# Start and tail of a two-problem attention kernel: x transposed on TensorE, a new order of the first projections and batches, more PSUM banks for the last output tiles

## The chip, the core and the metric

The kernel runs on one core of a Trainium2 chip. The metric is the time of one execution on the device in microseconds. Three runs of the kernel before took 801.57, 802.39 and 803.64 us; the median is 802.39. One execution was also recorded by the hardware profiler.

A core has five engines, each with its own instruction stream: TensorE (PE) multiplies matrices and writes to PSUM, VectorE (DVE) and ScalarE (ACT) read PSUM and compute, GpSimd (POOL) works in SBUF, and SyncE (SP) here only issues DMAs. PSUM has eight banks. A bank holds 128 x 512 numbers in f32. In the profile PEld is the loading of a matmul's stationary operand.

## The reference

Two independent problems, A and B, have the same shapes. For each of them, in bf16:

```python
B, Sq, D = 16, 80, 576
Hq, Hkv, Sk, Dh = 32, 16, 512, 128
q = (x @ wq).reshape(B, Sq, Hq, Dh).transpose(0, 2, 1, 3)
k = jnp.repeat(k_cache, 2, axis=1)
v = jnp.repeat(v_cache, 2, axis=1)
scores = jnp.einsum("bhqd,bhkd->bhqk", q, k) * (Dh ** -0.5)
p = softmax(scores, axis=-1)
o = jnp.einsum("bhqk,bhkd->bhqd", p, v)
result = o.transpose(0, 2, 1, 3).reshape(B, Sq, Hq * Dh) @ wo
```

The two results are joined along the last axis. Softmax goes over 512 keys, and two query heads share one key head.

## The kernel before, in words

**Units.** Work is cut into 128 units `U`, 64 a problem. A unit is one batch (80 rows of x) and four key heads, thus eight query heads. Eight units make an octet `goct` with one piece of 1024 columns of wq. A problem has four pieces `q` and two halves of eight batches (640 rows of x, `half` 0 and 1), so eight octets. The order is problem, piece, half, batch.

**Steps of a unit.** Q projection (line 454): for each of an octet's eight heads `i`, five matmuls over the depth of x give the transposed Q of up to six batches at a time. In octet 0 a head is cut into batches 0 and 1 (`c` = 0, 160 columns) and the other six (`c` = 1, 480 columns). In later octets the cut is six batches and then two. ACT or DVE moves the result to `qT` (465, 466). Scores: each key head has 160 query rows. The first 128 go through one matmul of 512 keys (558). The 32 rows left over of the four heads are packed side by side into one bank by four column-tiled matmuls (544, `qkr`). So a unit has five score tiles, k = 0 being the packed one. DVE takes the maximum (567), ACT the exponential and the row sum (571), DVE one reciprocal for a unit (577), POOL multiplies (580), PE transposes the tile with four matmuls (586), DVE moves it to `pT` (592, 594), PE multiplies by V (624) and ACT moves the result to `oT` (639).

**Pairs.** `qk_order` (496 to 500) puts units in groups of `GR` = 2: first the packed tiles of both, then the four tiles of the first and of the second. One `qkr` operation holds the packed matmuls of both units, so it waits for both K loads.

**Output.** After two pieces of wq the product with 16 heads of wo is formed: 20 tiles of 128 x 288, sixteen matmuls each, in two operations of eight (669). For the first two pieces ACT copies a tile to `acc` (681). For the last two DVE adds tile and `acc` into one of two `osb` slots (696), and SP writes it to the result (702). All these tiles use the one PSUM bank of class `M`.

**Loads.** SP issues x by transposing DMAs straight into `xT` (390 and 395; a half is split into rows 0 to 159 and 160 to 639, and each part into four chunks of depth and a last one), K by transposing DMAs into six slots (513), V into four (517), wo in four pieces (490), and the later wq. ACT issues the wq of octet 0 in two pieces of 512 columns (428, 431).

**What sets the order.** Every operation has a stream, an engine, a key and an assumed duration. The planner (`_Sched.arrange`, 97) simulates the engines with these durations. Each time an engine is free it takes, among the heads of its streams that are ready in the simulation, the one with the lowest key. It also hands out PSUM banks: from the class's list in `BANKS` (25) it takes the one that became free first. The resulting order on each engine is fixed in the program; on the chip every operation waits on semaphores for its real inputs. Before all this, PE runs eight matmuls on constants (`em_warm`, 361).

In octet 0 the keys let all eight `c` = 0 groups go first, then the `c` = 1 groups mixed with the first groups of octet 1, which read half 1 of x.

Of the kernel before, what the change touches and what calls it, by code (L numbers as in the profile page):

```python
# [6 lines left out]
BF16 = mybir.dt.bfloat16  # L7
F32 = mybir.dt.float32
AF = mybir.ActivationFunctionType
AX = mybir.AxisListType  # L10

GR = 2
LA = 9
NK = 6
# [5 lines left out]
QSH = 10  # L20
NOC = 2
NOSB = 2
NWARM = 8
NWC = 4
BANKS = dict(S=(0, 1, 2, 6), T=(3, 4), O=(5,), M=(7,), M0=(7, 5, 6, 3, 4), M1=(7, 6))
XDMA = True
RG = ((0, 1, 2, 3, 4),)
NSS = 6
OPSPLIT = 2
OP0 = 20.0  # L30
OPS = 1.25
LP0 = 20.0
# [6 lines left out]
def _mm(n, cols):  # L39
    return n * (cols * MM1 + MM0)  # L40
# [239 lines left out]
def bass_concat_heads__gqa_block_cached__gqa_block_cached__near_ridge_kernel(  # L280
# [5 lines left out]
    probs = [  # L286
        (A_x, A_k_cache, A_v_cache, A_wq, A_wo),
        (B_x, B_k_cache, B_v_cache, B_wq, B_wo),
    ]
    B, SQ, D = A_x.shape  # L290
    _, G, SK, DH = A_k_cache.shape
# [4 lines left out]
    NPP = B // 8  # L296
    NG = 2 * NOCT * NPP
    UPR = NOCT * NPP * 8
    NSU = 2 * UPR
# [3 lines left out]
    NROW = 8 * SQ  # L303
    NRT = NROW // 128
# [3 lines left out]
    with ExitStack() as es:  # L308
# [3 lines left out]
        ones = sb("ones", [128, 128], BF16)  # L312
# [26 lines left out]
        def R(res, ver):  # L339
            return (res, ver)  # L340
# [26 lines left out]
        def em_warmend(e):  # L367
# [3 lines left out]
        S.add("pe", -990, em_warm, reads=[R(("ones",), 0), R(("warm",), 0)], writes=[R(vw, 0)],  # L371
              name="warm", stream="W", dur=NWARM * 0.427, alloc=[vw])
        S.add("dve", -980, em_warmend, reads=[R(vw, 0)], writes=[R(("warm",), 1)], name="warmend", stream="warmset")
        IDENT = R(("ident",), 0)

        def unit(g):
# [1 line left out]
            q, half = divmod(r, NPP)  # L378
            return prob, q, half

        XB = ((0, 160), (160, 640))
        for prob in range(2):
            x_ap = probs[prob][0]
            for half in range(NPP):
                for part in range(2):
                    r0, r1 = XB[part]

                    def em_ldx(e, x_ap=x_ap, half=half, r0=r0, r1=r1):
                        src = x_ap.rearrange("b s d -> (b s) d")[half * NROW + r0:half * NROW + r1, :]
                        return e.dma_start_transpose(xT[:, half, 0:4, r0:r1],  # L390
                                                     src[:, 0:512].rearrange("n (c d) -> n c d", c=4))

                    def em_ldx4(e, x_ap=x_ap, half=half, r0=r0, r1=r1):
                        src = x_ap.rearrange("b s d -> (b s) d")[half * NROW + r0:half * NROW + r1, :]
                        return e.dma_start_transpose(xT[:, half, 4:5, r0:r1],  # L395
                                                     src[:, D - 128:D].rearrange("n (c d) -> n c d", c=1))

                    k_ = 5.0 * (prob * UPR + 8 * half - QSH) - 20.0 + 0.2 * part
                    if prob == 0:
                        k_ = ((-100.0, -60.0), (-45.0, -44.9))[half][part]  # L400
                    nr = (r1 - r0) / 640.0
                    S.add("sp", k_, em_ldx, writes=[R(("xT", half, part, 0), prob)], dsem="d_x%d%d" % (half, part),
                          name="ldx%d.%d.%d" % (prob, half, part), stream="x", dur=4.4 * nr + 0.3, cost=3.5 * nr)
                    S.add("sp", k_ + 0.01, em_ldx4, writes=[R(("xT", half, part, 1), prob)],
                          dsem="d_x%d%d" % (half, part), name="ldx4%d.%d.%d" % (prob, half, part), stream="x",
                          dur=1.1 * nr + 0.3, cost=0.9 * nr)

        QB = ((0, 6), (6, 2))
        for goct in range(NG):
# [30 lines left out]
            for i in range(8):  # L440
                for c in range(2):
                    if goct == 0:
                        b0, nb = ((0, 2), (2, 6))[c]
                        x = (-LA - 6.0 + 0.6 * i) if c == 0 else (-LA + 0.5 + 1.2 * i)
                    else:
                        b0, nb = QB[c]
                        x = 5.0 * (u0 - QSH + i) + (3.6 if c == 0 else 1.6)
                    n0, n1 = b0 * SQ, (b0 + nb) * SQ
                    vb = S.bank("M0" if goct == 0 else "M1" if goct == 1 else "M")

                    def em_qp(e, i=i, wsl=wsl, half=half, n0=n0, n1=n1, vb=vb):
                        last = None
                        for ck in range(5):
                            last = e.matmul(ps[:, vb.phys, 0:n1 - n0],  # L454
                                            lhsT=wq_sb[:, wsl, ck, i * 128:(i + 1) * 128],
                                            rhs=xT[:, half, ck, n0:n1], start=(ck == 0), stop=(ck == 4))
                        return last

                    col = (i // 2) * 160 + (i % 2) * 80

                    def em_qev(e, en, qsl=qsl, b0=b0, nb=nb, n0=n0, n1=n1, col=col, vb=vb):
                        dst = qT[:, qsl, b0:b0 + nb, col:col + 80]
                        src = ps[:, vb.phys, 0:n1 - n0].rearrange("p (b s) -> p b s", b=nb)
                        if en == "act":
                            return e.activation(dst, src, AF.Identity, scale=SCALE)  # L465
                        return e.tensor_scalar(dst, src, SCALE, None, op0=AluOpType.mult)  # L466

                    xr = [R(("xT", half, p_, h_), prob) for p_ in range(2) for h_ in range(2)
                          if n0 < XB[p_][1] and n1 > XB[p_][0]]
                    S.add("pe", x, em_qp,  # L470
                          reads=[R(("wq", wsl, s_, i // 4), wv) for s_ in "ab"] + [R(("wqz",), 0)] + xr,
                          writes=[R(vb, 0)], name="qp%d.%d.%d" % (goct, i, c), stream="Q",
                          dur=_mm(5, n1 - n0), lat=0.2, alloc=[vb])
                    big = n1 - n0 > 200
                    S.add(("act", "dve"), x + 0.4, em_qev, reads=[R(vb, 0)],
                          writes=[R(("qT", qsl, bl, i), goct) for bl in range(b0, b0 + nb)],
                          name="qev%d.%d.%d" % (goct, i, c), stream="qev",
                          dur=dict(act=0.47, dve=0.57) if big else dict(act=0.21, dve=0.23))
# [15 lines left out]
                          dsem="d_wo", name="ldwo%d.%d.%d" % (prob, hh, wc), stream="wo", dur=0.5, cost=2.0)  # L494

        qk_order = []
        for p_ in range(NSU // GR):
            qk_order += [(GR * p_ + j_, 0) for j_ in range(GR)]
            qk_order += [(GR * p_ + j_, k_) for j_ in range(GR) for k_ in range(1, 5)]
        Qof = dict((uk, i_) for i_, uk in enumerate(qk_order))  # L500
        vbs = {}
        group = []
# [1 line left out]
        for U in range(NSU):  # L504
# [10 lines left out]
            def em_ldv(e, vc_ap=vc_ap, b=b, q=q, vs=vs):  # L515
                src = vc_ap[b, 4 * q:4 * q + 4, :, :].rearrange("g (p j) d -> p g (j d)", j=4)
                return e.dma_start(v_sb[:, vs, :, :], src)

            S.add("sp", 5.0 * (U - U % GR) + 0.5 * (U % GR) - LA - 8.0, em_ldk, writes=[R(("kT", ks), U)],
                  dsem="d_k%d" % ks, name="ldk%d" % U, stream="K", dur=3.4, cost=2.75)  # L520
            S.add("sp", 5.0 * U - 6.0, em_ldv, writes=[R(("V", vs), U)],
                  dsem="d_v%d" % vs, name="ldv%d" % U, stream="V", dur=0.45, cost=1.6)
# [2 lines left out]
            for k in range(5):  # L525
# [10 lines left out]

                if k == 0:
                    group.append((U, vb, ks, qsl, bl, goct))
                    if len(group) == GR:
                        def em_qkr(e, group=tuple(group)):  # L540
                            last = None
                            for _, vb_, ks_, qsl_, bl_, _ in group:
                                for g4 in range(4):
                                    last = e.matmul(ps[32 * g4:32 * g4 + 32, vb_.phys, :],  # L544
                                                    lhsT=qT[:, qsl_, bl_, g4 * 160 + 128:g4 * 160 + 160],
                                                    rhs=kT[:, ks_, :, g4 * 128:(g4 + 1) * 128],
                                                    start=True, stop=True, tile_position=(0, 32 * g4))
                            return last

                        S.add("pe", Qof[(group[0][0], 0)] - LA + 0.0, em_qkr,  # L550
                              reads=[R(("qT", g_[3], g_[4], i), g_[5]) for g_ in group for i in (1, 3, 5, 7)]
                              + [R(("kT", g_[2]), g_[0]) for g_ in group],
                              writes=[R(g_[1], 0) for g_ in group], name="qkr%d" % U, stream="S",
                              dur=GR * (_mm(1, 512) + 0.0105), lat=0.2, alloc=[g_[1] for g_ in group], mode=1)
                        group = []
                else:
                    def em_qk(e, gl=gl, vb=vb, ks=ks, qsl=qsl, bl=bl):
# [89 lines left out]
        for prob in range(2):  # L647
            for hh in range(NPAIR):
                for half in range(NPP):
                    for n in range(NB_):  # L650
# [6 lines left out]
                        else:  # L657
                            x = 5.0 * (base + OP0 + OPS * (half * NB_ + n)) + 0.6
                        slot = (half * NB_ + n) % NOSB
                        vb = S.bank("M")  # L660
                        ver = (prob, hh)
                        ot_reads = [R(("oT", half, b_, q_, pr_), ver) for b_ in bls for q_ in range(2)
                                    for pr_ in range(2)]
# [15 lines left out]
                        if hh == 0:  # L679
                            def em_ea(e, rb=rb, c3=c3, vb=vb):  # L680
                                return e.copy(acc[:, rb, c3 * DC:(c3 + 1) * DC], ps[:, vb.phys, 0:DC])

                            S.add("act", xe, em_ea, reads=[R(vb, 0)],
                                  writes=[R(("acc", rb, c3), ver)], name="oea%d.%d.%d" % (prob, half, n),
                                  stream="oea", dur=0.30)
                        elif not last:
                            def em_em(e, rb=rb, c3=c3, vb=vb):
# [94 lines left out]
```

## Time and profile before

| What | us |
|---|---|
| median of three runs | 802.39 |
| the profiled execution's own time | 802.79 |
| its span, first to last instruction | 801.0 |
| PE busy (8200 matmuls) | 783.7 (98%) |
| DVE busy | 685.3 (86%) |
| ACT busy | 614.4 (77%) |
| POOL busy | 431.9 (54%) |
| PE's mean granted clock | 0.998 of full speed |
| DMA queues' packets, share of 16 engines | about 89% |
| first projection / first score on PE starts at | 8.81 / 25.89 |
| last unit's transposes, last V product end near | 778.4 / 780.2 |

Matmuls are pipelined, and their ends are modelled: a busy PE is not always a PE at its peak. The chain of work that ended last is followed back from the last instruction, and its pieces, in order of time, show what the end had to wait for. Where it passes through PE, the pieces show the pace of matmuls that follow one another closely. A list of waits names the engine that waited, whom it waited for, the total, the number of times and the longest, in us. SP's own timeline shows how long each DMA kept SP in issuing, which is not the time until it lands.

### The profile page before, as it was taken

Reading aid. Unit: us, or ns where it says so; the run is one execution under the profiler, and the core shown is the slowest. Engines: PE = TensorE matmul, PEld = TensorE weight load, DVE = VectorE, ACT = ScalarE, POOL = GpSimd, SP = SyncE. Lnnn points to the kernel's source line nnn. Section 1 sums busy time; section 2 is a strip of 40 time slices with the busy share of each in tenths; the row PEclk is TensorE's granted clock in tenths of the full one; section 3 lists DMA queues with packets and bytes.
Section 4 is the critical chain, followed back from the end, with each engine's and each line's share of the span. In section 5 each row is a group of like instructions: output and inputs, shape, how many; then the busy total and the mean of one; then the engine's idle time right before and its main releaser. Section 6 shows DMA issues by size and latency. Waiting matters only on the chain.

```text
span 801.0 us, 21485 instructions
## 1 busy us (share of the span) xinstructions
PE 783.7 (98%) x8200; PEld 575.3 (72%) x8200; DVE 685.3 (86%) x1533; ACT 614.4 (77%) x1750; POOL 431.9 (54%) x647
## 2 busy tenths in 40 slices
PE   6999999999999999999999999999999999999997
PEld 3567766777777777776777777777777777777784
DVE  1899999878878899988888899988897888998971
ACT  0699979778787789876777778978787877987850
POOL 1366666555454656655554646755564645665650
PEclk9999999999999999999999999999999999999999
DMA  8999999999689899999997979998886977997411
GB/s 183 240 252 213 255 246 220 255 215 211 159 160 229 193 229 213 223 214 217 229 201 183 232 183 255 224 244 208 156 188 137 197 166 196 257 231 194 142 43 30
DMA packets 366917, 160.73 MB, mean 201 GB/s; under 512 B 282784, under 2 KB 362784, under 8 KB 366816
## 3 DMA queue, kind: packets, MB, share of 16 engines
q1 hardware_dynamic: 365600, 158.17, 88.2%
q8 instruction: 67, 1.10, 0.6%
q10 hardware_dynamic: 1216, 1.18, 0.6%
q14 instruction: 34, 0.28, 0.1%
HBM read 85.98 MB, written 2.95 MB: 111 GB/s over the span
## 4 chain that ended last, share of the span: by engine, by line
PE 85%; DVE 10%; SPq 2%; ACT 1%; DMA 1%; POOL 0%; issue 0%; DVEq 0%
PE ps L669 19%; PE ps L454 19%; PE ps L624 16%; PE ps L586 16%; PE ps L558 11%; DVE negmax L567 6%; PE ps L544 4%; DVE pT L594 2%; SPq L390 1%; ACT p_sb L571 1%; DVE qT L466 1%; DVE pT L592 1%; DMA xT<-in_A_x_dram 1%; SPq L395 1%; DVE osb L696 0%; DMA out_dram<-osb 0%
## 5 line engine op out<-in xcount | busy, mean ns | idle before, releaser
L580 POOL TENSOR_SCALAR p_sb<-p_sb,rinv 128x512 bf16<-128x512 bf16 x640 | 429.5, 692 | 343.9 <-DVE rinv L577 343.6
L571 ACT ACTIVATE p_sb<-ps,negmax 128x512 bf16<-128x512 f32 x640 | 442.3, 696 | 81.3 <-DVE negmax L567 77.1
L567 DVE TENSOR_REDUCE negmax<-ps 128x1 f32<-128x512 f32 x640 | 426.7, 679 | 8.0 <-PE ps L558 4.8
L586 PE MATMUL ps<-ident,p_sb 128*128 128x128 bf16 x2560 | 238.7, 220 | 1.5 <-DVE pT L592 0.7
L594 DVE COPY pT<-ps 128x512 bf16<-128x512 bf16 x512 | 207.7, 414 | 26.8 <-PE ps L586 23.4
L454 PE MATMUL ps<-xT,wq_sb 128*128 128x480 bf16 (+1 forms) x1280 | 217.2, 304 | 7.7 <-DMA xT<-in_A_x_dram 6.5
L624 PE MATMUL ps<-pT,v_sb 128*128 128x160 bf16 x2048 | 217.8, 233 | 0.6 <-ACT oT L639 0.5
L586 PEld LDWEIGHTS ps<-ident,p_sb 128*128 128x128 bf16 x2560 | 178.3, 98 | 38.1 <-DVE pT L594 6.7
L624 PEld LDWEIGHTS ps<-pT,v_sb 128*128 128x128 bf16 x2048 | 155.6, 98 | 67.6 <-issue 20.2
L558 PE MATMUL ps<-kT,qT 128*128 128x512 bf16 x512 | 186.0, 380 | 0.4 <-ACT p_sb L571 0.3
L669 PE MATMUL ps<-wo_sb,oT 128*128 128x288 bf16 x1280 | 174.8, 286 | 3.3 <-DVE osb L696 3.3
L454 PEld LDWEIGHTS ps<-xT,wq_sb 128*128 128x128 bf16 x1280 | 109.6, 100 | 65.6 <-DMA xT<-in_A_x_dram 7.8
L639 ACT CAST oT<-ps 128x320 bf16<-128x320 f32 x256 | 110.0, 430 | 51.1 <-PE ps L624 50.2
L669 PEld LDWEIGHTS ps<-wo_sb,oT 128*128 128x128 bf16 x1280 | 121.9, 98 | 36.9 <-DVE osb L696 5.3
L571 ACT ACTIVATION_READ_ACCUMULATOR p_sb<-ps,negmax 128x1 f32 x640 | 132.8, 208 | 0.0
L465 ACT ACTIVATE qT<-ps 128x160 bf16<-128x160 f32 (+1 forms) x173 | 69.9, 404 | 24.4 <-PE ps L454 23.5
L466 DVE TENSOR_SCALAR qT<-ps 128x480 bf16<-128x480 f32 (+1 forms) x83 | 48.5, 584 | 27.7 <-PE ps L454 25.3
L592 DVE COPY pT<-ps 128x512 bf16<-128x512 bf16 x128 | 53.3, 416 | 2.9 <-PE ps L586 1.8
L558 PEld LDWEIGHTS ps<-kT,qT 128*128 128x128 bf16 x512 | 48.1, 98 | 4.1 <-ACT p_sb L571 1.5
L696 DVE TENSOR_TENSOR osb<-ps,acc 128x288 bf16<-128x288 f32 x40 | 18.3, 457 | 32.7 <-PE ps L669 31.3
L544 PE MATMUL ps<-kT,qT 128*32 128x512 bf16 x512 | 39.4, 384 | 0.0
L577 DVE RECIPROCAL rinv<-rowsum 128x5 f32<-128x5 f32 x128 | 23.1, 180 | 10.8 <-ACT p_sb L571 10.8
(14 smaller groups left out, 32.5 us busy)
## 6 DMA issues: line engine op xcount, KB each, us to landing
v_sb<-in_A_v_cache_dram SPq DMA_DIRECT2D x64, 512.0 KB, 4.8
v_sb<-in_B_v_cache_dram SPq DMA_DIRECT2D x64, 512.0 KB, 4.4
wo_sb<-in_A_wo_dram SPq DMA_DIRECT2D x8, 576.0 KB, 7.3
wo_sb<-in_B_wo_dram SPq DMA_DIRECT2D x8, 576.0 KB, 7.2
wq_sb<-in_B_wq_dram SPq DMA_DIRECT2D x4, 1024.0 KB, 7.1
wq_sb<-in_A_wq_dram SPq DMA_DIRECT2D x3, 1024.0 KB, 6.9
out_dram<-osb SPq DMA_DIRECT2D x40, 72.0 KB, 2.4
wq_sb<-in_A_wq_dram ACTq DMA_DIRECT2D x2, 512.0 KB, 5.1
```

The costliest lines, as they stand in the source:

```text
L454: last = e.matmul(ps[:, vb.phys, 0:n1 - n0], lhsT=wq_sb[:, wsl, ck, i * 128:(i + 1) * 128], rhs=xT[:, half, ck, n0:n1], start=(ck == 0), s ...
L465: return e.activation(dst, src, AF.Identity, scale=SCALE)
L544: last = e.matmul(ps[32 * g4:32 * g4 + 32, vb_.phys, :], lhsT=qT[:, qsl_, bl_, g4 * 160 + 128:g4 * 160 + 160], rhs=kT[:, ks_, :, g4 * 128: ...
L558: return e.matmul(ps[:, vb.phys, :], lhsT=qT[:, qsl, bl, gl * 160:gl * 160 + 128], rhs=kT[:, ks, :, gl * 128:(gl + 1) * 128], start=True, ...
L567: return e.tensor_reduce(negmax[:, si:si + 1], ps[:, vb.phys, :], axis=AX.X, op=AluOpType.max, negate=True)
L571: return e.activation(p_sb[:, psl, :], ps[:, vb.phys, :], AF.Exp, bias=negmax[:, si:si + 1], scale=1.0, accum_out=rowsum[:, ss, k:k + 1])
L580: return e.tensor_scalar(p_sb[:, psl, :], p_sb[:, psl, :], rinv[:, ss, k:k + 1], 1.0, op0=AluOpType.mult, op1=AluOpType.mult)
L586: last = e.transpose(psb[:, vt.phys, j * 128:(j + 1) * 128], p_sb[:, psl, j * 128:(j + 1) * 128], ident[:])
L594: return e.tensor_copy(pT[:, pts, gl, :, 0:128], psb[:, vt.phys, 0:512].rearrange("p (j n) -> p j n", j=4))
L624: last = e.matmul(ps[:, vo.phys, off:off + 160], lhsT=v_sb[:, vs, gl, j * 128:(j + 1) * 128], rhs=pT[:, pts, gl, j, :], start=(j == 0), st ...
L639: return e.copy(dst, src)
L669: last = e.matmul(ps[:, vb.phys, 0:DC], lhsT=oT[:, hi, rb * 128:(rb + 1) * 128], rhs=wo_sb[:, hi, c3 * DC:(c3 + 1) * DC], start=(hi == 0), ...
```

## The change

Four things are changed.

1. **x of problem A.** Four plain DMAs bring x as it lies in memory into the storage of `acc`, seen as bf16 (row blocks of 128; two blocks and then three for each half). For each of the ten blocks PE makes five 128 x 128 transposes into one PSUM bank, and DVE copies 128 x 640 into `xT`. A second run of eight matmuls on constants (`em_warm2`) stands after the first two blocks. The blocks of half 1 have keys that mix them with the projections. Problem B keeps the transposing DMAs, with a half in one part.
2. **Early projections.** In octet 0 heads 0 to 3 (first weight piece) come first, both cuts, then heads 4 to 7.
3. **First units unpaired.** Groups of one, one, and then two units.
4. **Last output tiles.** In problem B's last round, tiles 12 to 19 take their bank from five banks (class `ML`).

```diff
+GRP = (1, 1, 2)
 GR = 2
...
+NWARM2 = 8
...
+BANKS = dict(S=(0, 1, 2, 6), T=(3, 4), O=(5,), M=(7,), M0=(7, 5, 6, 3, 4), M1=(7, 6),
+             ML=(7, 5, 6, 0, 1))
+NML = 12
...
+XLD = ((-100.0, -60.0), (-25.0, -24.9))
+XH = -14.0
...
+        S.add("pe", -LA - 13.2, em_warm2, reads=[R(("ones",), 0), R(("warm",), 1)], writes=[R(vw2, 0)],
+              name="warm2", stream="X", dur=NWARM2 * 0.3, alloc=[vw2])
...
-                    k_ = 5.0 * (prob * UPR + 8 * half - QSH) - 20.0 + 0.2 * part
-                    if prob == 0:
-                        k_ = ((-100.0, -60.0), (-45.0, -44.9))[half][part]
...
+        xs = acc[:].bitcast(BF16)
+        XP = ((0, 2), (2, 5))
+        XA = -LA - 14.0
+        for half in range(NPP):
+            x_ap = probs[0][0]
+            for part, (k0, k1) in enumerate(XP):
+                def em_ldx(e, x_ap=x_ap, half=half, k0=k0, k1=k1):
+                    src = x_ap.rearrange("b s d -> (b s) d")[half * NROW + k0 * 128:half * NROW + k1 * 128, :]
+                    return e.dma_start(xs[:, half * NRT + k0:half * NRT + k1, 0:D],
+                                       src.rearrange("(k p) d -> p k d", p=128))
...
+            for blk in range(NRT):
+                rb = half * NRT + blk
+                vb = S.bank("M0" if half == 0 else "M1")
+                x = (XA + 0.5 * blk if blk < 2 else XA + 4.0 + 0.5 * blk) if half == 0 else XH + 0.8 * blk
+
+                def em_xtr(e, rb=rb, vb=vb):
+                    last = None
+                    for ck in range(5):
+                        c0 = ck * 128 if ck < 4 else D - 128
+                        last = e.transpose(psb[:, vb.phys, ck * 128:(ck + 1) * 128], xs[:, rb, c0:c0 + 128], ident[:])
+                    return last
+
+                def em_xev(e, half=half, blk=blk, vb=vb):
+                    return e.tensor_copy(xT[:, half, :, blk * 128:(blk + 1) * 128],
+                                         psb[:, vb.phys, 0:640].rearrange("p (c n) -> p c n", c=5))
...
+                S.add("dve", x + 0.3, em_xev, reads=[R(vb, 0)], writes=[R(("xT", half, blk), 0)],
+                      name="xev%d" % rb, stream="xev", dur=0.45, lat=0.13)
...
-                        x = (-LA - 6.0 + 0.6 * i) if c == 0 else (-LA + 0.5 + 1.2 * i)
+                        x = -LA - ((6.0, 3.6), (1.2, 0.5))[i // 4][c] + (0.6 if i < 4 else 0.05 if c == 0 else 1.2) * (i % 4)
...
-        for p_ in range(NSU // GR):
-            qk_order += [(GR * p_ + j_, 0) for j_ in range(GR)]
-            qk_order += [(GR * p_ + j_, k_) for j_ in range(GR) for k_ in range(1, 5)]
+        gsize, gfirst = {}, {}
...
+            n_ = min(GRP[i_] if i_ < len(GRP) else GR, NSU - u_)
...
-            S.add("sp", 5.0 * (U - U % GR) + 0.5 * (U % GR) - LA - 8.0, em_ldk, writes=[R(("kT", ks), U)],
+            S.add("sp", 5.0 * gfirst[U] + 0.5 * (U - gfirst[U]) - LA - 8.0, em_ldk, writes=[R(("kT", ks), U)],
...
-                        vb = S.bank("M")
+                        vb = S.bank("ML" if prob == 1 and last and half * NB_ + n >= NML else "M")
```

More of the change, by code (lines that the diff above doesn't have):

```diff
@@ L23 @@
 NWARM = 8
+NWARM2 = 8
 NWC = 4
-BANKS = dict(S=(0, 1, 2, 6), T=(3, 4), O=(5,), M=(7,), M0=(7, 5, 6, 3, 4), M1=(7, 6))
+BANKS = dict(S=(0, 1, 2, 6), T=(3, 4), O=(5,), M=(7,), M0=(7, 5, 6, 3, 4), M1=(7, 6),
+             ML=(7, 5, 6, 0, 1))
+NML = 12
 XDMA = True
@@ L373, in bass_concat_heads__gqa_block_cached__gqa_block_cached__near_ridge_kernel, with em_warm2 @@
         S.add("dve", -980, em_warmend, reads=[R(vw, 0)], writes=[R(("warm",), 1)], name="warmend", stream="warmset")
+        vw2 = S.bank("M")
+        def em_warm2(e, vw=vw2):
+            last = None
+            for _ in range(NWARM2):
+                last = e.matmul(ps[:, vw.phys, :], lhsT=ones[:], rhs=warm[:], start=True, stop=True)
+            return last
+        S.add("pe", -LA - 13.2, em_warm2, reads=[R(("ones",), 0), R(("warm",), 1)], writes=[R(vw2, 0)],
+              name="warm2", stream="X", dur=NWARM2 * 0.3, alloc=[vw2])
+        S.add("dve", -LA - 13.1, em_warmend, reads=[R(vw2, 0)], writes=[R(("warm",), 2)], name="warmend",
+              stream="warmset")
         IDENT = R(("ident",), 0)
@@ L379, in unit @@
             return prob, q, half
[L381 to L396, printed above, removed]
-                    k_ = 5.0 * (prob * UPR + 8 * half - QSH) - 20.0 + 0.2 * part
-                    if prob == 0:
-                        k_ = ((-100.0, -60.0), (-45.0, -44.9))[half][part]
[L401 to L406, printed above, removed]
@@ new lines, in bass_concat_heads__gqa_block_cached__gqa_block_cached__near_ridge_kernel @@
+        xs = acc[:].bitcast(BF16)
[8 more added lines that the diff above has]
+                                       src.rearrange("(k p) d -> p k d", p=128))
+                S.add("sp", XLD[half][part], em_ldx,
+                      writes=[R(("xs", half * NRT + k_), 0) for k_ in range(k0, k1)], dsem="d_x%d%d" % (half, part),
+                      name="ldx%d.%d" % (half, part), stream="x", dur=0.5, cost=0.54 * (k1 - k0))
+            for blk in range(NRT):
[3 more added lines that the diff above has]
+                def em_xtr(e, rb=rb, vb=vb):
+                    last = None
+                    for ck in range(5):
+                        c0 = ck * 128 if ck < 4 else D - 128
+                        last = e.transpose(psb[:, vb.phys, ck * 128:(ck + 1) * 128], xs[:, rb, c0:c0 + 128], ident[:])
+                    return last
+                def em_xev(e, half=half, blk=blk, vb=vb):
+                    return e.tensor_copy(xT[:, half, :, blk * 128:(blk + 1) * 128],
+                                         psb[:, vb.phys, 0:640].rearrange("p (c n) -> p c n", c=5))
+                S.add("pe", x, em_xtr, reads=[R(("xs", rb), 0), IDENT], writes=[R(vb, 0)], name="xtr%d" % rb,
+                      stream="X", dur=_mm(5, 128), lat=0.2, alloc=[vb])
+                S.add("dve", x + 0.3, em_xev, reads=[R(vb, 0)], writes=[R(("xT", half, blk), 0)],
+                      name="xev%d" % rb, stream="xev", dur=0.45, lat=0.13)
@@ new lines, in bass_concat_heads__gqa_block_cached__gqa_block_cached__near_ridge_kernel, with em_ldxt, em_ldxt4 @@
+        for half in range(NPP):
+            x_ap = probs[1][0]
+            def em_ldxt(e, x_ap=x_ap, half=half):
+                src = x_ap.rearrange("b s d -> (b s) d")[half * NROW:(half + 1) * NROW, :]
+                return e.dma_start_transpose(xT[:, half, 0:4, :], src[:, 0:512].rearrange("n (c d) -> n c d", c=4))
+            def em_ldxt4(e, x_ap=x_ap, half=half):
+                src = x_ap.rearrange("b s d -> (b s) d")[half * NROW:(half + 1) * NROW, :]
+                return e.dma_start_transpose(xT[:, half, 4:5, :],
+                                             src[:, D - 128:D].rearrange("n (c d) -> n c d", c=1))
+            k_ = 5.0 * (UPR + 8 * half - QSH) - 20.0
+            S.add("sp", k_, em_ldxt, writes=[R(("xT", half, b_), 1) for b_ in range(NRT)], dsem="d_x%d0" % half,
+                  name="ldxt%d" % half, stream="x", dur=4.7, cost=3.5)
+            S.add("sp", k_ + 0.01, em_ldxt4, writes=[R(("xT", half, "t"), 1)], dsem="d_x%d0" % half,
+                  name="ldxtb%d" % half, stream="x", dur=1.4, cost=0.9)
@@ L466, in em_qev @@
                         return e.tensor_scalar(dst, src, SCALE, None, op0=AluOpType.mult)
-                    xr = [R(("xT", half, p_, h_), prob) for p_ in range(2) for h_ in range(2)
-                          if n0 < XB[p_][1] and n1 > XB[p_][0]]
+                    xr = [R(("xT", half, b_), prob) for b_ in range(n0 // 128, (n1 - 1) // 128 + 1)]
+                    if prob:
+                        xr.append(R(("xT", half, "t"), 1))
                     S.add("pe", x, em_qp,
@@ L496, in bass_concat_heads__gqa_block_cached__gqa_block_cached__near_ridge_kernel @@
         qk_order = []
-        for p_ in range(NSU // GR):
-            qk_order += [(GR * p_ + j_, 0) for j_ in range(GR)]
-            qk_order += [(GR * p_ + j_, k_) for j_ in range(GR) for k_ in range(1, 5)]
+        gsize, gfirst = {}, {}
+        u_ = 0
+        while u_ < NSU:
+            i_ = len(set(gfirst.values()))
+            n_ = min(GRP[i_] if i_ < len(GRP) else GR, NSU - u_)
+            for j_ in range(n_):
+                gfirst[u_ + j_], gsize[u_ + j_] = u_, n_
+            qk_order += [(u_ + j_, 0) for j_ in range(n_)]
+            qk_order += [(u_ + j_, k_) for j_ in range(n_) for k_ in range(1, 5)]
+            u_ += n_
         Qof = dict((uk, i_) for i_, uk in enumerate(qk_order))
@@ L538, in bass_concat_heads__gqa_block_cached__gqa_block_cached__near_ridge_kernel @@
                     group.append((U, vb, ks, qsl, bl, goct))
-                    if len(group) == GR:
+                    if len(group) == gsize[U]:
                         def em_qkr(e, group=tuple(group)):
@@ L553, in bass_concat_heads__gqa_block_cached__gqa_block_cached__near_ridge_kernel @@
                               writes=[R(g_[1], 0) for g_ in group], name="qkr%d" % U, stream="S",
-                              dur=GR * (_mm(1, 512) + 0.0105), lat=0.2, alloc=[g_[1] for g_ in group], mode=1)
+                              dur=len(group) * (_mm(1, 512) + 0.0105), lat=0.2, alloc=[g_[1] for g_ in group], mode=1)
                         group = []
@@ L683, in bass_concat_heads__gqa_block_cached__gqa_block_cached__near_ridge_kernel @@
                             S.add("act", xe, em_ea, reads=[R(vb, 0)],
-                                  writes=[R(("acc", rb, c3), ver)], name="oea%d.%d.%d" % (prob, half, n),
+                                  writes=[R(("acc", rb, c3), ver)] + ([] if prob else [R(("xs", rb), c3 + 1)]),
+                                  name="oea%d.%d.%d" % (prob, half, n),
                                   stream="oea", dur=0.30)
```

## The prediction

> **What bounds the kernel now.** First the page: TensorE (PE) is busy in every slice but the first and the last, and the chain of work that ended last lies 85% on it.
>
> ```profile
> PE   6999999999999999999999999999999999999997
> ...
> PE 85%; DVE 10%; SPq 2%; ACT 1%; DMA 1%; POOL 0%; issue 0%; DVEq 0%
> ```
>
> So a saving has to make PE do less, start earlier or end without holes. The whole list of PE's waits names the two places worth the most (total us, times, longest):
>
> ```profile
> PE ps L454 <- DMA xT<-in_A_x_dram: 6.5, 2, 4.0
> PE ps L669 <- DVE osb L696: 3.3, 6, 0.6
> ```
>
> Then the chain in order of time (start, duration) at the start, and SP's own queue beside it:
>
> ```profile
> 13.24 4.32 DMA xT<-in_A_x_dram
> 17.56 0.05 issue
> 17.60 8.38 PE ps L454 x40
> ```
>
> ```profile
> 0.80 1.32 SPq L390 DMA_TRANSPOSE xT<-in_A_x_dram  x1
> ...
> 13.24 1.27 SPq L395 DMA_TRANSPOSE xT<-in_A_x_dram  x1
> 14.55 9.78 SPq L513 DMA_TRANSPOSE kT<-in_A_k_cache_dram  x4
> ```
>
> SP spends 0.80 to 14.51 issuing eight transposing loads of x; K comes behind them. PE, in its fixed order, stands at a projection of half 1 until the last of them lands at 17.6. The first scores start at 25.89. The groups by shape in 0 to 26 us give PE's useful work before that: 10 projections of 160 columns and 7 of 480. At full rate the chain prices them at 0.34 us (128.19) and 1.01 us (107.44) a group of five, together 3.4 + 7.1 = 10.5 us. So 25.95 - 10.5 = **15.5 us of PE's start are lost**.
>
> The tail, from the chain: the last seven output tiles have one PSUM bank, so each waits for the eviction of the one before.
>
> ```profile
> 779.65 0.55 PE ps L624 x8
> 780.20 2.15 PE ps L669 x16
> 782.35 0.02 issue
> 782.37 0.47 DVE osb L696
> 782.84 0.05 issue
> 782.89 2.15 PE ps L669 x16
> ```
>
> In between PE is full: if I count matmuls in stretches and price them by the chain (0.22 for four transposes, 0.28 for four of line 624, 0.98 for eight of line 669, 0.215 for a score), the work fills each stretch from 140 to 780 us to within 0.8 us in 20. Only 100 to 140 leaves 3.5 us open, and there the chain passes through ACT and DVE. From 26 to 100 us DVE is full as well:
>
> ```profile
> 60.00:100.00 40.00, 39.63 (x440) 28.49 (x438) 39.87 (x95) 38.50 (x112) 26.79 (x40) 1.00 1.05 234
> ```
>
> (PE, PEld, DVE, ACT, POOL busy, clock, DMA share, GB/s.) A head start must hold for both engines.
>
> **The change, part by part.** *Tail.* Seven tiles at a period of 782.89 - 780.20 = 2.69 us. With five banks in turn the next tile's matmuls follow at once; the period is then 2 x 0.98 = 1.96 us (the 2.15 of an isolated tile holds its drain). Six gaps x 0.73 = **4.4 us**; the floor is the 0.55 us that PE is seen idle, 6 x 0.55 = 3.3. DVE's 0.47 a tile fits. Next late would be the two osb slots: eviction 0.47, issue 0.43, landing 1.6 (the eight output DMAs after 780) make 2.5 us for two tiles, 1.25 each, below 1.96. Banks 6, 0 and 1 have held no scores since 772.4, and the planner takes the bank free longest, so bank 5 is not taken from the last PV group. What follows the last matmul stays.
>
> *Start, loads.* Eight transposing issues on SP become four plain ones. Plain loads on SP cost 0.57 each (line 517: 1.13 for two), so x ends near 0.8 + 4 x 0.57 = 3.1 instead of 14.51: K0 to K3 and V move up by some 11.4 us. On the DMA engines 1.47 MB of x, 1.18 MB of wq (ACT's queue, unmoved) and then K0 share one stream. Between 2.5 and 3.6 us the DMA engines, mostly on plain wq, moved 319 to 393 GB/s; from first bytes near 1.9 us, at 350 GB/s, both queues' 2.65 MB are through by 9.5. The first x part (0.29 MB, beside as much wq) is through at 3.6 and signals near 5; estimates from those rows. Bounds for it: not before 0.8 + 1.6 (the shortest output DMA), not after the 8.81 of today. K0, 0.5 MB issued at 3.1, lands some 5.2 after its turn near 9: 14.
>
> *Start, PE.* Transposing x adds 50 transposes: line 586's 0.22 for four gives 2.8 us. Warm2's eight 128x512 matmuls cost 8 x 0.215 = 1.7 at the score's price, 3.6 at line 364's. The chip row for a slow clock: the five-matmul 480-column projections that began at 18.64 have weight loads 0.40 apart until 20.59 and 0.20 after, so after an idle stretch about 3 us run at half rate. I charge one such stretch, 1.7 us (bounds: 0, as warm may have done it; 3.4, twice). Evictions of x: 128x640 bf16 from line 594's 414 ns for 512 scales to 0.52 (bounds 0.41, and 0.66 as the 480-column f32 row); ten are 5 us of DVE, which today is idle 80% of 0 to 15 us. They are PE's new waits: behind a late one stand the projections, and with them the scores; five banks hide most, and I charge 0.5 us (0 to 1.5). PE then runs from 5.2: 5.2 + 2.8 + 1.7 + 1.7 + 0.5 = 11.9 us lost, in place of 15.5: **3.6 us gained**. Cross-check in time: by its keys, eight 160s and five 480s (7.8 us) stand ahead of the first scores, which so start near 5.2 + 6.7 + 7.8 = 19.7, six us earlier, with 2.7 us less of projections done; the same 3.6. On DVE the lead is 6 us, less about 2 us of evictions not yet done (four, shared with ACT): above PE's, so PE decides.
>
> Here a rule speaks against the change. The Trainium skill, "TensorE: Matmul & The Clock Gate", Part 4, says that transposes do not count as busy for the clock. By it the clock could fall back between warm2 and the projections and the sum would lose another 1.7 us; Part 1 there puts warming at some 3.4 us of sustained matmuls, near the 3 us of the row. The trace's own transposes run at 55 ns, but always between other matmuls, so it does not decide.
>
> *Projections by landed weights.* The four heads of the second weight piece go behind six groups of the first. No count changes; today nothing waits for weights (projections of the second piece ran from 11.5, as soon as their turn came), so nothing by itself; it costs nothing while piece two lands (near 10) before PE reaches it (near 15). That margin covers a late landing of 5 us.
>
> *Unpaired first batches.* One more column-tiled group: the mode switch is not seen apart (eight small matmuls take 0.55, and the next score follows within 0.1), so -0.1 to 0.2, taken as 0.1. U0's softmax no longer waits for K1's first score, a wait that PE's spare projections covered; 0.
>
> *x of the second problem.* Eight transposing issues on SP between 302 and 357 us become four larger ones, the same bytes, 13.0 us of issue today. K and V behind them are prefetched up to six and four batches, some 5 to 6 us each, so 0; if that cover were gone, one 2 to 4 us block. PE's waits list none on in_B_x. `acc` as x's staging: its first write is at 132.8, so 0.
>
> *The middle.* The planner redoes the whole order. The hole of 100 to 140 sits beside the first four wo loads (91.94) and an 8.4 us K issue (94.37): K's lead is thin there, and an earlier K stream should widen it. Bounds: all 3.5 gained; or 3.5 lost, a second such hole. I take 0.4, near today's order.
>
> Sum: 4.4 + 3.6 - 0.1 + 0.4 = **8.3 us**. The profiled execution took 802.79 (span 801.0, 1.8 outside), so 794.5. It lies 0.4 above the median of 802.39: I predict **794.1**.
>
> **Rivals.** *Given back* (tail alone): PE's lead ends at the DVE-bound stretch, or the start is lost to bank waits and a cold clock; 802.39 - 4.4 = 798.0, with the 3.3 floor 799.1. For: DVE is full for 75 us. Against: DVE starts earlier too.
>
> *The middle closes as well*: the hole of 100 to 140 goes, 3.1 more than taken: 791.0. For: K moves up 11.4 us, PE only 6. Against: the six K slots cap the lead.
>
> *The banks do nothing*: the planner repeats one bank, or output DMAs limit: 798.5. Against: the slot count above.
>
> *Slower: the four wo stalls.* Four times wo's loads go ahead of K on SP (from 91.94, 290, 485, 677). The first costs 3.5 us; the stretches around the others show 0.4 to 0.5 each. If the new order leaves K late at all four, as it is at the first, the three others cost 3.1 more each, 9.3 us: 803.4, cancelling everything; with the first doubled too, 806.9. It makes the change slower by 0.3% only once these stalls take over 8.3 + 2.4 = 10.7 us. Against: K is issued earlier, not later.
>
> **How the numbers follow.** What a measurement of this kernel can tell is 0.3%, 2.4 us: faster is below 800.0, slower above 804.8. Forecast (792 to 797): 0.58. Middle closes (below 792): 0.12. Given back, or banks idle (797 to 800): 0.18. Stalls or a late start eat it (within 0.3%): 0.07. Slower: 0.05. So faster 0.88, same 0.07, slower 0.05. The range takes 790.5 (middle closes and a warm clock) to 799.1 (tail's floor).
>
> **What would show it.** Right: SP's first K issue near 3; PE's first x transposes near 5 and no wait on a load of x after it; first scores at 19 to 21 instead of 25.89; output tiles at 1.96 us with no wait on osb. Wrong: first scores after 23, half-rate projections for over 4 us, PE idle in 100 to 140 above 4 us, new holes near the wo loads, or osb waiting on output DMAs.

## The result and the profile after

The changed kernel takes 795.51 us (median of 4 runs, 794.05 to 796.39), the kernel before, run beside it, 803.01 (4 runs). The ratio is 0.9903, 95% interval 0.9876 to 0.9931: 7.8 us faster, between 5.5 and 10. The forecast was 794.1 in 790.5 to 799.1. The profiled execution took 794.05 us, its span 792.3.

PE's first slice, 6 before, now reads 9 (the runs on constants count in it), and the chain that ended last lies a little more on PE:

```profile
PE   9999999999999999999999999999999999999998
...
PE 88%; DVE 8%; DMA 1%; ACT 1%; POOL 1%; issue 0%
```

Both waits that the prediction read are gone from the list of PE's waits; what stands first is the start of the program:

```profile
PE ps L370 <- DVE warm L363: 1.2, 1, 1.2
PE ps L676 <- DMA v_sb<-in_A_v_cache_dram: 0.9, 2, 0.5
PE ps L638 <- POOL p_sb L632: 0.9, 3, 0.4
```

SP's timeline after (start, duration): four plain loads, K at once behind them, then the first V.

```profile
0.79 2.49 SPq L407 DMA_DIRECT2D acc<-in_A_x_dram  x4
3.33 15.92 SPq L565 DMA_TRANSPOSE kT<-in_A_k_cache_dram  x4
19.29 1.13 SPq L569 DMA_DIRECT2D v_sb<-in_A_v_cache_dram  x2
```

The same two loads of V before:

```profile
24.37 1.13 SPq L517 DMA_DIRECT2D v_sb<-in_A_v_cache_dram  x2
```

The first K goes out 11.2 us earlier, but four K issues now take 15.92 us instead of 9.78, so V goes out only 5.1 us earlier.

The chain in order of time: line 370 is the first run on constants, 422 the transposes of x, 385 the second run, 498 the projections, 596 the first scores.

```profile
1.24 3.59 PE ps L370 x8
4.84 1.07 PE ps L422 x10
5.90 2.04 PE ps L385 x8
7.95 0.84 PE ps L422 x15
8.78 1.04 PE ps L498 x15
...
14.60 3.41 PE ps L498 x30
18.01 0.33 PE ps L596 x4
```

Up to the first scores PE runs without a wait on any load, and they start at 17.9 instead of 25.9. At the end, PE's timeline has one block of seven tiles:

```profile
775.28 0.72 PE L676 MATMUL ps<-pT,v_sb 128*128 128x160 bf16 x8
775.83 13.88 PE L721 MATMUL ps<-wo_sb,oT 128*128 128x288 bf16 x112
```

and DVE evicts one every 1.96 us:

```profile
778.00 0.46 DVE L749 TENSOR_TENSOR osb<-ps,acc 128x288 bf16<-128x288 f32 x1 [2.06 <-PE ps L721]
779.95 0.46 DVE L749 TENSOR_TENSOR osb<-ps,acc 128x288 bf16<-128x288 f32 x1 [1.50 <-PE ps L721]
```

So both ends are as planned. The middle is not. I count PE's loss by stretches as the prediction did: length, less the stretch's matmuls at the chain's full-rate prices (for a 480-column projection matmul 0.202 us, a 160-column one 0.068). Constants and transposes of x count as loss. The first row is a sum of four windows, and a matmul across an edge counts in both; in one window the row is 0.6 to 1.0 higher in every column, and the gain below is then 3.9.

| us lost by PE in | before | five banks alone, two profiles | after, three profiles | after, wo held back |
|---|---|---|---|---|
| 0 to 60 | 16.7 | 15.3, 15.4 | 11.8, 12.4, 12.1 | 11.9 |
| 60 to 100 | 1.4 | 1.1, 1.3 | 5.5, 6.3, 6.0 | 2.4 |
| 100 to 140 | 4.2 | 3.8, 4.0 | 2.3, 3.0, 1.9 | 1.4 |
| 140 to 770 | 8.4 | 7.1, 6.7 | 6.9, 7.2, 6.7 | 6.9 |
| to 770 in all | 30.7 | 27.3, 27.4 | 26.5, 28.9, 26.7 | 22.5 |

The start is 3.7 us better by 60 us (means 15.8 and 12.1), and between 60 and 100 a new loss of 4 to 5 us takes it. To 770 us the changed kernel is 1.1 us ahead (means 28.5 and 27.4). Busy time hides this: in 60 to 100 PE of the changed kernel still counts 37.67 of 40 us as busy.

### The profile page after: what moved, and what is told of

Read it like the earlier page. It is cut to its first block, busy times and chain, and to the rows that moved or that the text cites. A ratio compares the mean times of both kernels' runs of the same rounds, so it can differ in the third digit from the quotient of the medians.

```text
span 792.3 us, 21596 instructions
## 1 busy us (share of the span) xinstructions
PE 784.6 (99%) x8258; PEld 577.2 (73%) x8258; DVE 689.4 (87%) x1539; ACT 616.1 (78%) x1755; POOL 432.0 (55%) x647
## 4 chain that ended last, share of the span: by engine, by line
PE 88%; DVE 8%; DMA 1%; ACT 1%; POOL 1%; issue 0%
PE ps L721 20%; PE ps L498 19%; PE ps L676 17%; PE ps L638 16%; PE ps L610 12%; DVE negmax L619 5%; PE ps L596 4%; DVE pT L646 2%; DMA v_sb<-in_A_v_cache_dram 1%; DVE qT L510 1%; ACT p_sb L623 1%; POOL p_sb L632 1%; DVE pT L644 0%; PE ps L370 0%; PE ps L422 0%; PE ps L385 0%
## 5 line engine op out<-in xcount | busy, mean ns | idle before, releaser
L498 PE MATMUL ps<-xT,wq_sb 128*128 128x480 bf16 (+1 forms) x1280 | 214.4, 300 | 1.1 <-DVE qT L510 0.5
L498 PEld LDWEIGHTS ps<-xT,wq_sb 128*128 128x128 bf16 x1280 | 106.5, 98 | 57.3 <-issue 3.4
L509 ACT ACTIVATE qT<-ps 128x160 bf16<-128x160 f32 (+1 forms) x178 | 70.7, 397 | 19.4 <-PE ps L498 18.6
L629 DVE RECIPROCAL rinv<-rowsum 128x5 f32<-128x5 f32 x128 | 22.9, 179 | 11.2 <-ACT p_sb L623 11.2
```

What stands on the lines that cost most here:

```text
L498: last = e.matmul(ps[:, vb.phys, 0:n1 - n0], lhsT=wq_sb[:, wsl, ck, i * 128:(i + 1) * 128], rhs=xT[:, half, ck, n0:n1], start=(ck == 0), s ...
```

## The experiments

All but those that say otherwise start from the changed kernel. Ratios are to the kernel before on the same chip. A changed key or bank makes the planner lay out the whole order anew, so each part's edit was also followed through the stretches above. Two orders did stay: the five banks alone give, on each engine, the same instructions in the same order as before, and the changed kernel without the five banks the same as with them.

**Five banks alone** (on the kernel before):

```diff
+                        vb = S.bank("ML" if prob == 1 and last and half * NB_ + n >= NML else "M")
```

> The kernel before with only the five banks for the last eight output tiles. Theory (the parts add up; the tail is six gaps of 0.73 us): 4.4 us faster than before, a ratio of 0.9945, tiles at 1.96 us, nothing else moved up to the last unit. Rival (most of the 7.5 us comes from the start and the new order, the banks little): under 2 us.

Measured: 795.62 us against 801.73, ratio 0.9934 (0.9921 to 0.9947). The tail from the first of the seven tiles to the end of the last eviction is 14.4 us (776.47 to 790.85) instead of 18.75 (780.20 to 798.95): 4.4 us, as worked out. Both ends, first the last eviction before, then the tiles and the last eviction here:

```profile
798.49 0.46 DVE L696 TENSOR_TENSOR osb<-ps,acc 128x288 bf16<-128x288 f32 x1 [2.23 <-PE ps L669]
```

```profile
776.47 13.88 PE L671 MATMUL ps<-wo_sb,oT 128*128 128x288 bf16 x112
790.39 0.46 DVE L698 TENSOR_TENSOR osb<-ps,acc 128x288 bf16<-128x288 f32 x1 [1.50 <-PE ps L671]
```

The tiles also begin 3.7 us earlier than in the profile of before, though the order is the same: two executions differ by that much. The banks are the largest part.

**The rest without the five banks** (`vb = S.bank("M")`):

> The changed kernel with the last tiles back on one bank. Theory: it gives back 4.4 us, so it is 3 to 4 us faster than before (ratio 0.9955), with the tail of before, period 2.69 us. Rival (start is worth nothing by the end, all is tail): equal to before within 1 us.

Measured: 798.5 us, ratio 0.9970 (0.9959 to 0.9982). 2.4 us faster than before by the ratio, 3.2 by the medians: at or below the 3 to 4 expected, above nothing. The period is again 2.69. The changed kernel's three ratios (0.9903, and 0.9933 and 0.9910 below) average 0.9915, so here too the banks are worth about 4.4 us.

**x by transposing DMAs, all the rest changed** (the kernel before with the other three parts):

> All of the change but the first part: x of both problems by transposing DMAs as before, with the new order of the first projections, the unpaired first units and the five banks. Theory (the start's gain comes from x off SP's queue): K is issued near 14.5 as before, first scores not before 21, 4.4 us from the tail and 0 to 2 from the order: ratio 0.992 to 0.9945. Rival (the order alone, which no longer asks for half 1 early, gives the start's gain): within 1 us of the changed kernel, ratio 0.990.

Measured: 796.29 us, ratio 0.9938 (0.9913 to 0.9962), no better than the five banks alone. Its six runs spread widely, from 793.8 to 799.7, and the profile is of one at 799.1: first scores at 20.2 (expected not before 21), but PE waits 3.8 us for x and 4.4 us for V. Without the plain loads the new order shows no gain that this spread lets one see.

**Old keys of the first projections** (`x = (-LA - 6.0 + 0.6 * i) if c == 0 else (-LA + 0.5 + 1.2 * i)`):

> The changed kernel with the old keys of the first projections: all eight narrow groups, then the wide ones mixed with those of half 1. Theory (PE is full from 4.7 us on in either order, the second weight piece and half 1 have landed by 10): the same total within 1 us, first scores earlier than 17.9 but with fewer projections done. Rival (the order by landed weights carries part of the gain): 2 us or more slower than the changed kernel, with PE idle on a landing before 15 us.

Measured: 795.99 us, ratio 0.9938 (0.9926 to 0.9951). Beside the average of 0.9915 this would make the old keys 1.8 us slower, but no changed kernel ran in this group, and its 0.9933 (0.9919 to 0.9946) in the next is not to be told apart. So whether the expectation of no difference held is open. Scores start at 15.1, but PE waits 1.2 us before the blocks of half 1, whose load lands at 11.6, not by 10. From the chain:

```profile
2.34 9.29 DMA acc<-in_A_x_dram
11.63 0.14 issue
11.77 0.44 PE ps L422 x5
```

By 60 us PE has lost 13.5 us, 1.4 more than with the new keys. From 60 to 100 it then loses 4.2 us, against 5.5 to 6.3, and by 140 us the two are level (20.6 and a mean of 20.4).

**The changed kernel again:**

> The changed kernel again, as the reference of this group. Theory (two parts that add: the tail 4.4 to 6 us, the start 2.4 to 3.6 us): a ratio of 0.990, 8 us faster than before. Rival (the start is not worth anything beyond the tail): 0.993, as with the five banks alone.

Measured: 795.41 us, ratio 0.9933 (0.9919 to 0.9946): the rival's number.

**All units in pairs** (`GRP = ()`):

> The changed kernel with all units in pairs again. Theory (one column-tiled group more or less, and a softmax whose delay PE's spare projections cover): the same as the changed kernel within 1 us. Rival (the first unit alone is what lets the scores start at 18): PE waits for K1's landing, first scores 2 to 4 us later, 2 us or more slower than the changed kernel.

Measured: 796.06 us, ratio 0.9942 (0.9924 to 0.9959), beside 0.9933 not to be told apart. First scores at 18.6.

**Without the second run on constants** (`em_warm2` and its `em_warmend` removed):

> The changed kernel without the second run of matmuls on constants. Theory from the trace (the clock rose inside that run, near 6.4 us, and it took 2.25 us): without it PE waits for x's second part instead, and the projections start cold; first projection about 1 us earlier, 1 to 2 us of half rate after it, total the same within 1 us. Rival (transposes keep the clock up as well as matmuls): the start is 1.5 to 2 us shorter. Second rival (the clock falls back through the transposes): 2 us or more slower.

Measured: 794.46 us, ratio 0.9928 (0.9913 to 0.9944): the same within 1 us. PE waits for x's second part, and then works at half rate. From its timeline (fifteen transposes in 1.78 instead of 1.00 us):

```profile
4.63 1.27 PE L410 MATMUL ps<-ident,acc 128*128 128x128 bf16 x10
7.32 1.78 PE L410 MATMUL ps<-ident,acc 128*128 128x128 bf16 x15 [1.41 <-DMA acc<-in_A_x_dram]
8.89 2.41 PE L486 MATMUL ps<-xT,wq_sb 128*128 128x160 bf16 x20
```

The first projection starts at 8.89, not a microsecond before the 8.62 of the changed kernel, and the scores at 19.07 instead of 17.94; by the end nothing is left of it.

**Half of the V load of units 4 to 19** (the other half of their V keeps older values):

```diff
+                if 4 <= U < 20:
+                    return e.dma_start(v_sb[:, vs, :, 0:256], src[:, :, 0:256])
```

> The changed kernel with only half of the V load of units 4 to 19 (the other half keeps older values, so their output differs): 4 MB less for the DMA engines between 20 and 110 us. Theory (the 7 us that PE loses between 60 and 120 us is the K and V stream, too slow beside the loads of wq and wo): the loss falls to 2 to 4 us and the whole is 3 to 5 us faster than the changed kernel. Rival (the loss comes from the planned order and from DVE and ACT, and the DMA engines are only busy): the loss stays within 1 us.

Measured: 790.48 us, ratio 0.9873 (0.9857 to 0.9889), 4.9 us faster than the changed kernel in the same group. PE's loss in 60 to 120 is 4.9 us, more than the 2 to 4 expected; 3.7 of it lies in 60 to 80, right behind the wo loads, and from 80 on it is 1.3 (changed kernel, same group: 4.9). For units 13 to 19 V now lands 2.6 us and more before its first product, where the changed kernel has 0 to 2.1. This fits a K and V stream that sets the pace, but it does not rule out the planned order: the edit also gave the planner half the price for these loads, and PE's order differs from 61.4 us on. Windows of PE, PEld, DVE, ACT and POOL busy, clock, DMA share and GB/s, for 60 to 80 and 80 to 100:

```profile
60.00:80.00 20.00, 17.22 (x185) 12.04 (x183) 18.04 (x42) 17.73 (x52) 12.50 (x20) 1.00 1.05 239
80.00:100.00 20.00, 19.66 (x220) 14.01 (x224) 18.98 (x44) 17.67 (x53) 11.73 (x18) 1.00 1.12 222
```

**The changed kernel beside the five banks alone, on one chip:**

> The changed kernel, beside the five banks alone on the same chip. Theory now (the head start is given back between 60 and 120 us to the K and V stream; what stays is the tail): equal to the five banks alone within 1.5 us, ratio 0.993. Rival (the start keeps 2 to 3 us): 2 to 3 us faster than the five banks alone, ratio 0.990.

> The kernel before with only the five banks, again. Both theories: ratio 0.9935 to before, about 5 us.

Measured: 793.9 us, ratio 0.9910 (0.9897 to 0.9923), and 795.71 us, ratio 0.9928 (0.9916 to 0.9940). The start keeps 1.4 us, with overlapping intervals; together with the 2.4 us of the kernel without banks, it is small and probably not nothing.

**wo held until units 14 to 17.** The planner had moved the first wo loads to 48.9 us, although their first use is at 130.5. SP of the changed kernel:

```profile
48.91 1.60 SPq L535 DMA_DIRECT2D wo_sb<-in_A_wo_dram  x3
50.56 7.63 SPq L565 DMA_TRANSPOSE kT<-in_A_k_cache_dram  x1
...
58.85 0.52 SPq L535 DMA_DIRECT2D wo_sb<-in_A_wo_dram  x1
59.41 5.31 SPq L565 DMA_TRANSPOSE kT<-in_A_k_cache_dram  x1
```

Behind three of them K's issue takes 7.63 us, where the one before took 4.08, and V of unit 6 goes out behind that, at 58.23. It lands at 63.4, and its first product starts at 63.8. For units 6 to 10 V lands 0.3 to 0.8 us before its first product here; in the profile of before it landed 5.8 to 8.3 us ahead. V had lost its lead a little sooner: for unit 4 it goes out at 43.5, before at 42.2, although PE needs it 5.5 us earlier.

A read of a row sum, written late enough, holds the four loads back:

```diff
+                          reads=[R(("rs", (14 + wc) % NSS, 0), 14 + wc)] if prob == 0 and hh == 0 else [],
```

> The changed kernel with the first four loads of wo held until the scores of units 14 to 17 are done, so K and V go ahead of them at 50 us. Theory (wo in front of K is what slows the stream between 60 and 100): the loss of PE between 60 and 100 us falls from 5.5 to 6.3 us to 2 to 3; 2 to 3 us faster than the changed kernel. Rival (the stream lacks time as a whole up to the first output tiles, wherever wo lies in it): the loss moves behind 100 us and the total stays within 1 us.

Measured: 791.07 us, ratio 0.9880 (0.9863 to 0.9896), 2.4 us faster than the changed kernel in the same group (0.9910): the best version. SP now goes on with K and puts wo at 99:

```profile
49.57 0.58 SPq L570 DMA_DIRECT2D v_sb<-in_A_v_cache_dram  x1
50.20 3.46 SPq L566 DMA_TRANSPOSE kT<-in_A_k_cache_dram  x1
...
98.91 2.27 SPq L535 DMA_DIRECT2D wo_sb<-in_A_wo_dram  x2
```

The same stretch, in the changed kernel and then here; PE's matmuls are 395 and 431, its loss 5.5 and 2.4 us:

```profile
60.00:100.00 40.00, 37.67 (x395) 24.65 (x393) 37.95 (x87) 33.67 (x101) 25.19 (x39) 1.00 1.04 247
```

```profile
60.00:100.00 40.00, 38.76 (x431) 27.76 (x429) 38.70 (x92) 37.60 (x109) 26.42 (x41) 1.00 1.05 242
```

The DMA share is the same: the DMA engines are full either way, and what changed is the order of the loads. The loss did not move behind 100 us, as the rival would have it. One thing stays open. From 48.9 us on SP's order differs, and so PE's differs from 59.7 us on. The list of PE's waits held only 0.9 us for V, and how much of the loss was waiting and how much the order that the planner made around late loads, this run does not separate.

**wo held until units 18 to 21, output tiles later** (first round from 24 units on, 1.1 apart):

> As the one before, but wo is held until units 18 to 21 and the first round of output tiles starts four units later and goes a little denser (24 and 1.1 units in place of 20 and 1.25). Theory: with 2.4 MB of wo out of the stretch in which PE has no output tiles, its loss between 60 and 140 us falls to 3 to 4 us in all and the whole is 3 to 4 us faster than the changed kernel. Rival (without output tiles PE has less to fill its holes with, and denser tiles later press on the one bank): no faster than the changed kernel.

Measured: 794.96 us, ratio 0.9925 (0.9912 to 0.9938). The loss in 60 to 140 is 3.7 us as expected, but 140 to 200 loses 3.2 (0.5 otherwise), 2.5 of them PE waiting for V. The first tile starts at 148.7. No gain.

## Why the prediction was right, and which step was not

**Tail: right.** 4.4 us worked out, 4.4 in the traces. By time the five banks alone bring 5.3 and 5.8 us, with intervals from 4.2 to 6.7. The extra microsecond is not explained, as the order before the tail is the same; the clock, under *Sum*, is a hint.

**Start: right in size, its terms only roughly.** 3.6 expected, 3.7 by 60 us. At the first scores it was more: 17.94 less 7.8 of projections is 10.1 lost, not 11.9. x's first part was there by 4.6, the clock rose at about 6.4 inside the second run (0.8 lost instead of 1.7), and there were no bank waits. The first profile of before also had a late start for its order: the five banks alone, with the same order, had first scores at 23.5 (13.0 lost instead of 15.5). "K0 to K3 and V move up by some 11.4 us" held for K0 alone: K1 to K3 went out 4.8 to 6.2 us earlier, V 5.1.

**Projections by landed weights: not settled.** "No count changes ... so nothing by itself" left out that the old keys stand before half 1. Its last part landed at 11.6, not by 9.5. The new keys are worth 1.4 us by 60 us, nothing by 140, and the 1.8 by time compares groups.

**The middle: wrong, with its sign.** Taken as +0.4, it was about -2.6: between 60 and 140 PE loses 8.3 us (mean of three) instead of 5.3, and 0.5 comes back later. The step was "K's lead is thin there, and an earlier K stream should widen it". The stream began earlier, but the planner put four wo loads ahead of K at 49 to 59 us, over 70 us before their use. That it does so because SP is free sooner is inferred: in every version with the plain loads and wo not held, the first wo goes out at 40 to 52 us, and in x by transposing DMAs with all the rest changed at 93. In outcome this is most of the rival *given back* (by the traces 2.6 of 3.7 us), but not for its reason: DVE did not stop the lead, as the kernel with wo held back keeps it. The mechanism is that of the slower rival, a wo stall in the stream of K and V, at the first of four places only. Of the signs, those of being right came, the scores even earlier than 19 to 21, but so did one of being wrong: new holes near the wo loads. The stretches of 100 us around the other three lose 1.2 to 1.5 us, before 1.3 to 1.4.

**Unpaired units and problem B's x: nothing, as taken.** Pairs cannot be told apart; no wait on in_B_x appears.

**Sum.** 4.4 + 3.7 - 2.6 = 5.5 us by the traces; the three timings give 7.8, 5.4 and 7.2. That the first lies next to the forecast of 8.3 is partly luck: the middle took 3.0 us more than was put in for it, and beside this timing the kernel before ran at 803.01, against 801.73, 800.29 and 801.6 in the other groups. The forecast leaned on one profiled execution, and that one had lost 3.4 us more before 770 than two others with the same order.

Part of that is the clock. Windows of 15 to 22 us, behind PE's wait for x, before and then with the five banks alone in the same order (the clock is the number before the DMA share):

```profile
15.00:22.00 7.00, 4.50 (x19) 2.24 (x19) 2.04 (x4) 0.00 (x0) 0.00 (x0) 0.76 1.03 200
```

```profile
15.00:22.00 7.00, 5.36 (x30) 2.81 (x31) 3.37 (x6) 0.00 (x0) 0.00 (x0) 1.00 1.05 200
```

Of 39 runs of the kernel before in the three later groups, 28 have a mean granted clock below 1.000 (median 801.7 us) and 11 have 1.000 (800.3). All 14 runs of the changed kernel, which has no such long wait, have 1.000 (795.1). Beside runs at full clock the gain is thus 5.2 us, near the 5.5 of the traces. That the rest of the timed gain comes from the clock is not shown: no run changes it alone, and with the five banks alone the two kinds of run do not differ (795.6 and 795.7).

The rule weighed against the change, that transposes do not count as busy for the clock (the Trainium skill, "TensorE: Matmul & The Clock Gate", Part 4), cost nothing. Fifteen transposes directly after the second run took 0.84 us, full rate, and the projections behind them ran at full rate too; 0.84 us of them is too short to test it. The kernel without the second run speaks against it, in one execution: after a wait of 1.4 us PE began transposes at 7.32 and projections at 8.89, all at half rate, and full rate came at 10.6. Without the transposes that is 1.7 us of work, where projections alone, from 17.60 in the kernel before, took 3.0.

## What to carry to other kernels

When a change frees a queue early, look at what the planner will put into the space: a bulk load pulled far ahead of its use can stand before the stream that feeds the bound engine, and then an earlier start is given back. Count the bound engine's work by its matmuls in stretches, since its busy time hides a loss of 5 us in 40. Before trusting a sum of a few microseconds, compare two executions of the same program.

## What was not expected of the hardware

The same program, in two executions, left half rate at different times: in the profile after, ten transposes at 4.84 took 1.07 us, half rate; with wo held back, whose first instructions are the same, 0.55, full rate (4.57 to the next block at 5.12). It changed nothing by 18 us (first scores at 17.94 and 17.95), because PE then waited 0.77 us for x's second part. In one program x by transposing DMAs landed at 17.6 and in another execution of the same order at 16.6; together with a shorter time at half rate that moved the first scores by 2.4 us.
